# Attention scores of one unit split into products of 64 and of 16 contraction lanes

## The chip, the core and the metric

The kernel runs on one core of a Trainium2 chip. The metric is the device time of one execution in microseconds (us), the median of several runs. Five engines work beside each other, each with its own queue: TensorE (PE, matrix products; PEld is its weight load), VectorE (DVE), ScalarE (ACT), GpSimd (POOL) and SyncE (SP, which issues DMAs). Products land in PSUM, in banks of 512 float32 for each of the 128 partitions.

## What is computed

Routed attention, followed by a gated feed-forward layer. Queries, keys and values have 4 batches, 8 heads, 768 positions and 64 lanes. Each query and each key belongs to the nearest of 16 centroids of its head, and a query sees only keys of its own cluster:

```python
q_assign = np.argmax(np.einsum('bhsd,hcd->bhsc', q_n, c_n), axis=-1)
k_assign = np.argmax(np.einsum('bhsd,hcd->bhsc', k_n, c_n), axis=-1)
mask = q_assign[:, :, :, None] == k_assign[:, :, None, :]
scores = scale * np.matmul(q, k.transpose(0, 1, 3, 2))
scores = np.where(mask, scores, -1000000000.0)
scores = scores - np.max(scores, axis=-1, keepdims=True)
attn = np.exp(scores)
attn = attn / (np.sum(attn, axis=-1, keepdims=True) + 1e-09)
return np.matmul(attn, v).astype(np.float32)
```

The result, 3072 tokens of 512 lanes, is scaled by its root mean square and a weight, then goes through `silu(x @ w_gate) * (x @ w_val) @ w_out` with 1536 inner lanes.

## The kernel before

**The mask is inside the product.** A head's queries and keys are kept transposed as bf16, lanes on partitions, in the tiles `qext` and `kext`: 64 partitions (`D`) hold the lanes and the next 16 (`NC`) a one-hot vector of the cluster, so `KR = D + NC` = 80 partitions are contracted. The keys are divided by `ZS` = 2048 beforehand. So a query and a key of the same cluster get 1 added to their product, and the exponential, with scale `scale * ZS` and bias `off` = `-scale * ZS`, takes the 1 away where the clusters agree and leaves a very negative number where they don't.

**Units.** The work is cut into 8 units (`UNITS`, `NU` = 8), each one batch and one half of its queries: `UQ` = 384 query columns, all 8 heads, all 768 keys. `NU - 2` is number 6, the seventh.

**Scores.** `scores(u, h, i)` (L304) makes two of the six key blocks of 128 keys for one head; three calls make a head, 24 a unit. It takes a PSUM tile `s` of two banks (the pool `ps_s` has 2 such tiles), and for each bank issues one product with 128 keys as the stationary operand and 384 queries as the moving one (L314). One exponential on ScalarE (L318) then reads both banks and writes two blocks of `pT` in bf16.

**What follows.** `pv(u, h)` (L322) multiplies `pT` with the values and a column of ones (18 products of 65 columns, tile `acc`), and VectorE divides by the sum. The feed-forward of a unit runs one or two units later: `xtrans` (L371, tile `tx`), `gv` (L382, tiles `gate` and `val`, 4 products of 384 columns each), `out_mm` (L411, tile `o`, products of 512 columns).

**Order.** The order on each queue is written out by hand (`manual_schedule`). `attention` (L603) goes through the 24 score calls of a unit. After each call it puts what is due: the `pv` of the head before at a head's second call, squares for the norm in the last head, and pieces of a list `fill` in proportion to their estimated cost, so that TensorE has other products between two score calls. For the seventh unit the list holds the end of the feed-forward of unit 4, the output products of unit 4, and the first part of the feed-forward of unit 5; no group of heads is prepared any more. The first score call of each unit is followed by the second at once.

**Cluster products.** `cluster_products` (L235) multiplies queries or keys with the centroids in float32 for four heads; each product fills 32 of the array's columns and writes 32 partitions of the tile `sc` (L240). They occur up to the sixth unit.

**Names in the views.** `s` scores, `pT` exponentials, `acc` attention output, `gate`/`val`/`o` feed-forward, `tx` transposes of its input, `tq` transposes of queries and keys, `sc` cluster products.

Of the kernel before, what the change touches and what calls it, by code (L numbers as in the profile page):

```python
# [22 lines left out]
def kernel(  # L23
# [12 lines left out]
    nc = tc.nc  # L36
    B, H, S, D = q.shape
# [3 lines left out]
    P = 128  # L41
    ST = S // P
    HT = ST // 2
# [4 lines left out]
    NU = len(UNITS)  # L48
# [3 lines left out]
    KR = D + NC  # L52
# [55 lines left out]
    qext = [const.tile([P, HG, S], BF16, name=f"qext{i}") for i in range(4)]  # L108
    kext = [const.tile([P, HG, S], BF16, name=f"kext{i}") for i in range(4)]
# [38 lines left out]
    for i in range(P // 32):  # L148
        r = slice(32 * i, 32 * i + 32)
# [64 lines left out]
    def cols(of, g, e, a=0, b=UQ):  # L214

        return of.rearrange("p (x e) -> p x e", e=2)[:, a:b, e] if g < H // HG else of[:, e * UQ + a:e * UQ + b]
# [87 lines left out]
    def scores(u, h, i):  # L304
        b, col, nt = UNITS[u]
        g, hh, w = b * 2 + h // HG, h % HG, nt * P
        if i == 0:
            pT[u, h] = ptp.tile([P, ST, UQ], BF16, tag="pT", name="pT")
        n = ST // nt
        ps = ps_s.tile([P, 2, 512], F32, tag="s", name="s")  # L310
        flat = ps.rearrange("p a b -> p (a b)")
        for j in range(n):
            kc = n * i + j
            nc.tensor.matmul(ps[:, j, :w] if nt == HT else flat[:, j * w:(j + 1) * w],  # L314
                             lhsT=cols(kext[g % 4][:KR, hh], g, kc // HT, kc % HT * P, (kc % HT + 1) * P),
                             rhs=cols(qext[g % 4][:KR, hh], g, col // HT, 0, w), start=True, stop=True)
        of = ps[:, :, :w] if nt == HT else flat[:, :n * w].rearrange("p (c w) -> p c w", w=w)
        nc.scalar.activation(pT[u, h][:, n * i:n * i + n, :w], of, ACT.Exp, bias=off, scale=scale * ZS)  # L318
# [116 lines left out]
    def group_work(g):  # L435

        t, c = [], []
        for h in range(HG):
            n = g * HG + h
            t += [(0.3, lambda h=h: trans(g, h, 0)), (0.3, lambda h=h: trans(g, h, 1))]  # L440

            def others(n=n):
                vcast(n)
                load_qk(n + NQ)
                load_v(n + NV)

            def both(h=h, f=others):
                cast(nc.gpsimd, g, h, 0)
                f()
                cast(nc.vector, g, h, 1, (0,))  # L450
            if g == 2:
                c.append((0.0, others))
            else:
                c += [(0.0, both), (0.0, lambda h=h: cast(nc.vector, g, h, 1, (1,)))]
        a = []
        for m in range(2):
            a += [(0.0 if i else 0.7, f) for i, f in enumerate(cluster_steps(g, m))]
            if g <= 3:
                a.append((0.0, lambda m=m: place(nc.sync if g == 2 else nc.gpsimd, g, m)))
        if g > 3:  # L460
            a.append((0.0, lambda: [place(nc.gpsimd, g, m) for m in range(2)]))
        return t, c, a
# [17 lines left out]
    def ffn_work(u):  # L480
        n = UNITS[u][2] / HT
        w = [(0.18 * n, lambda c=c: xtrans(u, c)) for c in range(CC)]
        for f in range(FC):
            for val in (False, True):
                w.append((0.64 * n, lambda f=f, val=val: gv(u, f, val)))
        return w

    def out_work(u):
        return [(0.86, lambda t=t, p=p: out_mm(u, t, p)) for t in range(UNITS[u][2]) for p in range(3)]
# [113 lines left out]
    def attention(heads, fill, skip=0, hooks={}):  # L603
        gaps = [(u, h, i) for u, h in heads for i in range(UNITS[u][2])]
        total, done, n = sum(c for c, _ in fill), 0.0, 0
        for at, (u, h, i) in enumerate(gaps):
            scores(u, h, i)
            if i == min(1, UNITS[u][2] - 1):
                for p in due:
                    pv(*p)  # L610
                due[:] = [(u, h)]
            if h == H - 1:
                squares(u, i, False)
            if (u, h, i) in hooks:
                hooks[u, h, i]()
            while n < len(fill) and at >= skip and done <= total * (at + 1 - skip) / (len(gaps) - skip):
                done += fill[n][0]
                fill[n][1]()
                n += 1
        for _, f in fill[n:]:  # L620
            f()

    attention([(0, h) for h in range(H)], [], hooks={(0, *divmod(i, HT)): first.get(i, more) for i in range(H * HT)})
    for u in range(1, NU):
        ffn, o, g = ffn_work(u - 1), out_work(u - 2) if u > 1 else [], u + 2
        if u == 1:
            t, c, a = group_work(2)
            t3, c3, a3 = group_work(3)
            n = 4
# [61 lines left out]
```

## Time and profile before

| | |
|---|---|
| median of 3 runs | 354.11 us (354.07 to 354.23) |
| the profiled execution | 354.17 us |
| its span, first to last instruction | 352.4 us |
| mean granted TensorE clock | 0.995 |
| start of the first score of the seventh unit | 237.88 us |
| start of the first score of the eighth unit | 274.25 us |
| score products, all units | 384, of 80 lanes and 384 columns |
| exponentials | 192, 904 ns each |

A busy time counts an engine as busy from the start of an instruction to its end. Products on TensorE are pipelined, so one begins while the one before still drains: the duration of one (about 325 ns for 384 columns) is longer than the distance from one start to the next. A line of the groups gives the source line, engine and operation, written tile and read tiles, the shapes as partitions x elements with their type, how many there are, then their busy time, the mean duration of one in ns, and the idle time of the engine just before them with what ended it. A line of the timeline gives start, length from the first start to the last end, and then the same names.

### The profile page before, as it was taken

How to read it: one execution, taken by the hardware profiler on the slowest of the kernel's cores; microseconds unless marked ns; L12 is line 12 of the kernel's file. 1: busy time of each engine (PE TensorE's matmuls, PEld its weight loads, DVE VectorE, ACT ScalarE, POOL GpSimd, SP SyncE). 2: the span in 40 equal slices, each digit the busy share in tenths (PEclk: the TensorE clock that was granted, in tenths of full speed). 3: DMA queues.
4: the chain of work that ended last, by engine and by line, in shares of the span. 5: the costliest groups of instructions: out<-in, count | busy, mean ns of one | idle time of the engine just before them, and what ended most of it. 6: DMA issues, size and time to landing. Idle time of an engine off the chain costs nothing.

```text
span 352.4 us, 7991 instructions
## 1 busy us (share of the span) xinstructions
PE 340.9 (97%) x3028; PEld 210.2 (60%) x3045; DVE 223.1 (63%) x553; ACT 261.6 (74%) x459; POOL 110.2 (31%) x222
## 2 busy tenths in 40 slices
PE   8996999999999999999999999999999999999996
PEld 4544755664665656655576556756566656665653
DVE  4888678777457755686457863687456654666330
ACT  5995877986787777887688877978778887764421
POOL 4999168340542702444033711327000000000000
PEclk9998999999999999999999999999999999999999
DMA  7999959454253012610140011000010001001002
GB/s 270 368 206 171 274 141 250 139 172 146 74 175 95 24 59 86 192 34 16 60 123 2 17 38 60 2 2 23 32 61 0 2 33 60 2 1 62 30 2 89
DMA packets 27158, 31.62 MB, mean 90 GB/s; under 512 B 4464, under 2 KB 24176, under 8 KB 27120
## 3 DMA queue, kind: packets, MB, share of 16 engines
q1 hardware_dynamic: 18464, 25.02, 21.3%
q0 software_dynamic: 8368, 5.71, 9.9%
q8 instruction: 24, 0.39, 0.5%
q10 hardware_dynamic: 288, 0.39, 0.3%
q14 instruction: 14, 0.11, 0.1%
HBM read 28.35 MB, written 6.29 MB: 98 GB/s over the span
## 4 chain that ended last, share of the span: by engine, by line
PE 85%; DVE 7%; ACT 5%; issue 1%; POOL 0%; DVEq 0%; ACTq 0%; POOLq 0%
PE gate L390 17%; PE o L415 17%; PE val L390 16%; PE s L314 16%; PE acc L332 9%; PE tq L206 5%; PE sc L240 3%; ACT pT L318 3%; PE tx L377 1%; PE warm L117 1%; DVE kext L225 1%; ACT xn L357 1%; DVE qext L298 1%; DVE kext L298 1%; ACT th L398 1%
## 5 line engine op out<-in xcount | busy, mean ns | idle before, releaser
L318 ACT ACTIVATE pT<-s,off 128x768 bf16<-128x768 f32 x192 | 170.9, 904 | 38.0 <-PE s L314 36.8
L314 PE MATMUL s<-qext,kext 80*128 80x384 bf16 x384 | 95.1, 329 | 2.4 <-ACT pT L318 1.5
L399 DVE SCALAR_TENSOR_TENSOR th<-th,gate 128x384 f32<-128x384 f32 x84 | 46.4, 552 | 51.5 <-ACT th L398 51.4
L390 PE MATMUL gate<-xnT,wg 128*128 128x384 bf16 x384 | 78.3, 325 | 0.5 <-DVE gvT L403 0.4
L390 PE MATMUL val<-xnT,wv 128*128 128x384 bf16 x384 | 78.1, 326 | 0.0
L415 PE MATMUL o<-wo,gvT 128*128 128x512 bf16 x259 | 66.0, 379 | 0.9
L225 POOL CAST qext<-qkT 64x384 bf16<-64x384 f32 x64 | 34.1, 540 | 76.6 <-ACT qkT L212 37.3
L314 PEld LDWEIGHTS <-kext 80*128 80x128 bf16 x384 | 37.1, 99 | 33.4 <-issue 8.1
L398 ACT ACTIVATE th<-gate 128x384 f32<-128x384 f32 x84 | 41.1, 489 | 15.3 <-PE gate L390 14.9
L390 PEld LDWEIGHTS <-wv 128*128 128x128 bf16 x384 | 36.1, 97 | 25.1 <-issue 3.4
L390 PEld LDWEIGHTS <-wg 128*128 128x128 bf16 x384 | 35.9, 97 | 24.9 <-issue 3.4
L403 DVE SCALAR_TENSOR_TENSOR gvT<-th,val 128x384 bf16<-128x384 f32 x84 | 46.1, 549 | 7.2 <-PE val L390 2.6
L332 PEld LDWEIGHTS <-pT 128*128 128x128 bf16 x1152 | 43.9, 98 | 9.8 <-DVE x L339 1.1
L332 PE MATMUL acc<-vbf,pT 128*128 128x65 bf16 x1152 | 46.0, 194 | 0.7 <-DVE x L339 0.7
L415 PEld LDWEIGHTS <-gvT 128*128 128x128 bf16 x276 | 25.8, 97 | 25.1
L206 PE MATMUL tq<-ident_f,qk 128*128 128x128 f32 x192 | 31.4, 284 | 2.2 <-DVE qkT L210 2.1
L206 PEld LDWEIGHTS tq<-ident_f,qk 128*128 128x128 f32 x192 | 23.8, 145 | 8.8 <-DVE qkT L210 2.5
L212 ACT ACTIVATE qkT<-tq 128x384 f32<-128x384 f32 x56 | 26.1, 497 | 3.6 <-PE tq L206 3.0
L281 POOL DMA_DIRECT2D qext<-oh x40 | 19.1, 487 | 30.3 <-DVE oh L270 24.2
L378 DVE TENSOR_SCALAR xnT<-tx,gcol 128x384 bf16<-128x384 bf16 x32 | 11.9, 413 | 24.3 <-PE tx L377 24.3
L418 ACT COPY o_sb<-o 128x512 f32<-128x512 f32 x23 | 13.5, 585 | 17.4 <-PE o L415 17.4
L281 POOL DMA_DIRECT2D kext<-oh x40 | 19.1, 485 | 11.0 <-DVE oh L270 11.0
(74 smaller groups left out, 254.7 us busy)
## 6 DMA issues: line engine op xcount, KB each, us to landing
qk<-in_q_dram SPq DMA_DIRECT2D x32, 192.0 KB, 4.0
vs<-in_v_dram SPq DMA_DIRECT2D x32, 192.0 KB, 4.2
out_dram<-o_sb SPq DMA_DIRECT2D x23, 256.0 KB, 2.0
qk<-in_k_dram SPq DMA_DIRECT2D x30, 192.0 KB, 4.1
wg<-in_moe_w_gate_dram POOLq DMA_DIRECT2D x4, 384.0 KB, 7.0
wv<-in_moe_w_val_dram POOLq DMA_DIRECT2D x4, 384.0 KB, 8.7
wo<-in_moe_w_out_dram POOLq DMA_DIRECT2D x3, 512.0 KB, 5.6
qext<-oh POOLq DMA_DIRECT2D x40, 12.0 KB, 1.6
```

What stands on the lines that cost most here:

```text
L206: nc.tensor.transpose(ps[:, i * P:(i + 1) * P], qk[:, part, 2 * i:2 * i + 2].rearrange("p t d -> p (t d)"), ident_f)
L212: nc.scalar.activation(to, ps, ACT.Copy, scale=by)
L225: on.tensor_copy(to, of)
L281: on.dma_start(out=ext[D:D + NC, h, e * UQ:(e + 1) * UQ], in_=put[g, m][32 * h + e * NC:32 * h + (e + 1) * NC])
L314: nc.tensor.matmul(ps[:, j, :w] if nt == HT else flat[:, j * w:(j + 1) * w], lhsT=cols(kext[g % 4][:KR, hh], g, kc // HT, kc % HT * P, (kc ...
L318: nc.scalar.activation(pT[u, h][:, n * i:n * i + n, :w], of, ACT.Exp, bias=off, scale=scale * ZS)
L332: nc.tensor.matmul(acc[:, h % 2, t], lhsT=pT[u, h][:, kc, t * P:(t + 1) * P], rhs=vbf[g % 4][:, hh, kc % HT * 2 + kc // HT], start=kc == 0 ...
L390: nc.tensor.matmul(ps, lhsT=w[:, c, f * P:(f + 1) * P], rhs=xnT[u][:, c, :n], start=c == 0, stop=c == CC - 1)
L398: nc.scalar.activation(th, ps, ACT.Tanh, scale=0.5)
L399: nc.vector.scalar_tensor_tensor(th, th, 1.0, ps, op0=ALU.add, op1=ALU.mult)
L403: nc.vector.scalar_tensor_tensor(gvT[u][:, f, :n], gates[u], 0.5, ps, op0=ALU.mult, op1=ALU.mult)
L415: nc.tensor.matmul(outs[u], lhsT=gvT[u][:, f, t * P:(t + 1) * P], rhs=wo[:, f], start=f == 0, stop=f == FC - 1)
```

## The change

In `scores`, the seventh unit's products are taken apart along the contracted lanes. Where one product contracted all 80 partitions for a bank, there are now two that accumulate in it: one over partitions 0 to 63 (the lanes), one over 64 to 79 (the clusters). The order of the four products of a call alternates between the banks: lanes into bank 0, clusters into bank 1, then clusters into bank 0, lanes into bank 1. The first two clear their banks, the last two add. All other units keep the two products of 80 partitions. The operands, the PSUM tile and the exponential are the same.

```diff
         ps = ps_s.tile([P, 2, 512], F32, tag="s", name="s")
         flat = ps.rearrange("p a b -> p (a b)")
-        for j in range(n):
+        if u == NU - 2:
+            for a, b in ((0, D), (D, KR)), ((D, KR), (0, D)):
+                for j, r in enumerate((slice(*a), slice(*b))):
+                    kc = n * i + j
+                    nc.tensor.matmul(ps[:, j, :w], lhsT=cols(kext[g % 4][r, hh], g, kc // HT, kc % HT * P, (kc % HT + 1) * P),
+                                     rhs=cols(qext[g % 4][r, hh], g, col // HT, 0, w), start=a[0] == 0, stop=a[0] != 0)
+        for j in range(n if u != NU - 2 else 0):
             kc = n * i + j
```

## The prediction

> **What bounds the kernel now.** I read the page from the top, then only the stretch in which the seventh unit (u = 6, the number that `NU - 2` names) runs. First the busy shares and the slices:
>
> ```profile
> PE 340.9 (97%) x3028; PEld 210.2 (60%) x3045; DVE 223.1 (63%) x553; ACT 261.6 (74%) x459; POOL 110.2 (31%) x222
> PE   8996999999999999999999999999999999999996
> PE 85%; DVE 7%; ACT 5%; issue 1%; POOL 0%; DVEq 0%; ACTq 0%; POOLq 0%
> ```
>
> TensorE is full in nearly every slice and is 85% of the chain that ended last. A busy TensorE need not be at its peak, so I look at start times. The scores of the seventh unit start at 237.88 us and those of the eighth at 274.25 us. The table of windows for nearly this stretch, and the groups in it with shapes kept apart:
>
> ```profile
> 237.80:274.20 36.40, 36.24 (x335) 22.57 (x337) 21.94 (x55) 29.24 (x52) 6.85 (x15) 1.00 0.08 28
> L318 ACT ACTIVATE pT<-s,off 128x768 bf16<-128x768 f32 x25 | 22.3, 901 | 3.8 <-PE s L314 3.7
> L314 PE MATMUL s<-qext,kext 80*128 80x384 bf16 x48 | 11.7, 325 | 0.0
> L314 PEld LDWEIGHTS <-kext 80*128 80x128 bf16 x49 | 4.7, 98 | 3.7
> ```
>
> The columns of the first line are length, then busy time of PE, PEld, DVE, ACT and POOL, the granted clock, DMA share and GB/s. PE is busy 36.24 of 36.40 us at full clock; ACT has 7 us free and waits 3.7 us for the scores. So here an extra nanosecond on TensorE is an extra nanosecond of the span. The 325 ns of a score product is latency. What it costs is the distance to the next start, which the timeline shows:
>
> ```profile
> 240.45 0.49 PE L314 MATMUL s<-qext,kext 80*128 80x384 bf16 x2
> 240.78 0.81 PE L390 MATMUL gate<-xnT,wg 128*128 128x384 bf16 x4
> 241.43 0.81 PE L390 MATMUL val<-xnT,wv 128*128 128x384 bf16 x4
> ```
>
> Two scores take 0.33 us, four gates 0.65 us: 162 ns for each product of 384 columns, whether 80 or 128 lanes are filled. Neither the unit's 24 score calls nor what stands around them shows a gap worth naming, except two waits for ScalarE: 71 ns between the first two calls, and the larger one at the border to the eighth unit:
>
> ```profile
> 274.25 0.49 PE L314 MATMUL s<-qext,kext 80*128 80x384 bf16 x2
> 275.00 0.48 PE L314 MATMUL s<-qext,kext 80*128 80x384 bf16 x2 [0.26 <-ACT pT L318]
> ```
>
> Start to start it is 587 ns where 167 would do, so 420 ns are lost there. The chain runs over ACT from 270.70 to 274.96 us.
>
> The last view is the nearest thing to the change: the cluster products (L240), which use 32 of the array's columns at a time.
>
> ```profile
> 230.84 0.49 PE L314 MATMUL s<-qext,kext 80*128 80x384 bf16 x2
> 231.26 0.85 PE L240 MATMUL sc<-qkT,cblk 128*32 128x384 f32 x8
> 232.04 0.82 PE L390 MATMUL val<-xnT,wv 128*128 128x384 bf16 x4
> 232.70 0.49 PE L314 MATMUL s<-qext,kext 80*128 80x384 bf16 x2
> ```
>
> The single start times say more. Four of the eight start 6 to 7 ns apart and run together. From the last score to the first cluster product it is 253 ns instead of 162: 91 ns for going in. From the last cluster product it is 418 ns to the next gate or val product, where one such pass takes 326: 92 ns for coming out, and the product after that follows at 173 instead of 162, 11 ns more. The weight load of the first product on each side starts only 2 to 4 ns ahead of it; elsewhere it starts a whole product earlier. Float32 isn't the cause: from scores to the float32 transposes (L206) it is 161 ns, and from these to scores 109, their own pitch.
>
> **What the Trainium skill says.** "TensorEngine Tiling (Array Packing)", Tiling Modes, Key Properties: changing the tiling mode, not just the tile, drains TensorE. It lists tiles of 64 rows and of 32 rows as different modes, and 128 rows as a third. The trace agrees for columns (91 and 92 ns); for rows it shows nothing. "TensorE: Matmul & The Clock Gate", Part 3, says that products in different row groups run concurrently, starting about 4 ns apart; the trace shows this for column groups of one size (6 to 7 ns). The tiling page's Gotcha 1 (PSUM Pressure) says that different row tiles must not write one PSUM bank at the same time, which fits the alternation of banks in the change. The TensorE page, LDWEIGHTS: a load takes its time by columns, not by lanes. No form in the trace tests that; the 80-lane loads last 98 ns and the 128-lane ones 97.
>
> **The change part by part.** Before, a call issues two products of 80 lanes, one for each bank. Now it issues four: 64 lanes into bank 0, lanes 64 to 79 into bank 1, lanes 64 to 79 into bank 0, 64 lanes into bank 1. There are 24 calls: 8 heads of 3.
>
> - Passes. 48 products become 96, each still 384 columns wide. If they run one after another: 2 more of 162 ns = 324 ns a call.
> - Switches. 80 lanes fill more than 64 rows, so these scores run in the mode of the gate products (162 ns apart, no drain). 64 lanes ask for tiles of 64 rows, 16 lanes at 64 for tiles of 32. A call then goes 128, 64, 32, 32, 64, 128: four switches. None of this kind is in the trace. Bounds: 0 if rows need no drain, 103 if each costs what leaving the column mode costs with its slower second product. I take 91 for going in, 92 for each of the two inside, 103 for coming out: 378 ns a call.
> - Sum for a call: 702 ns; for 24 calls 16.85 us. The first two calls of the unit follow each other directly, in one mode, so one way out and in falls away: 194 ns. That leaves 16.66 us.
> - Weight loads: 48 more of about 98 ns. Behind a running product of 162 ns they cost nothing; at a switch the cover is gone, and the 91 to 103 ns measured there already contain it.
> - Waits. No wait is added in kind: the first product of a call waits for the exponential two calls before, as now. That exponential ended at least 594 ns ahead in all calls but the second. Everything later on TensorE's queue moves by the sum; ACT's exponential starts later with it and has slack. A slower call removes the 71 ns. In the last head, two calls after 270.70 us each give ACT 0.7 us more to catch up, so the 420 ns at the border vanish too. Together 0.49 us comes back; next late would again be the stream on TensorE.
> - No DMA, VectorE or GpSimd instruction changes; SP's and POOL's queues are not touched.
>
> 16.66 - 0.49 = 16.2 us. The profiled execution took 354.17 us (span 352.4, with 1.8 around it), which gives 370.4. The median of the runs is 354.11, so 370.3 us.
>
> **Rivals.**
> 1. Both row sizes count as one tiled mode and run together. Each pair then takes one pass plus about 7 ns, and only the ways in and out cost: 14 + 194 = 208 ns a call, 4.99 us in all, less 0.19 for the adjacent calls and 0.45 of waits: 4.35 us, 358.5 us. For it: concurrency in the cluster products, and the TensorE page's row groups. Against it: the sizes differ, and those products are of one size.
> 2. One mode, but no overlap: 324 + 194 = 518 ns a call, 12.43 - 0.19 - 0.49 = 11.75 us, 365.9 us. For it: score products of both sizes still stream from one queue in order. Against it: the column groups of the cluster products do overlap, and the TensorE page says the same of row groups.
> 3. No overlap, no drain for rows: 324 ns a call, 7.78 - 0.49 = 7.3 us, 361.4 us. For it: 80 lanes next to 128 cost nothing. Against it: both are 128-row work.
> 4. Not slower: the two row groups run together, and no drain is paid for row tiles. The place is the score call, and the price is about 14 ns a call: 0.34 us less some 0.1 of waits, 354.3 us, no change. It decides as long as the switches of a call stay under about 22 ns together: 24 x (14 + 22) = 0.86 us, less 0.02 for the adjacent calls and 0.14 of waits, is the 0.7 us that can be told from no change. A clear gain has little to come from: even perfect pairs leave two passes a call, as before, and the two waits hold 0.49 us in all. Against it: the 91 and 92 ns at the column mode.
>
> **How the numbers follow.** The forecast, serial with four switches, gets 0.50. Its own range is 367 (60 ns inside a call and at its ends instead of 92: 24 x 4 x 32 ns = 3 us less) to 371.5. Rival 1 gets 0.20, rival 2 0.10, rival 3 0.07, rival 4 0.08; 0.05 is left for switches dearer than any here. The range from 358.0 to 371.8 holds the forecast and rivals 1 to 3 and leaves out 0.13 or so. Differences under 0.2% (0.7 us) can't be told from none. Rival 4 is the only source of same or faster: 0.06 same, 0.02 faster, and 0.92 slower.
>
> **What would show it.** In the profile after, the score line should have 96 products in two forms, 64 and 16 lanes, in the seventh unit. Serial with switches: starts about 254 ns apart inside a call except the middle pair at 162, and a weight load only a few nanoseconds ahead of its product. Rival 1: starts in pairs a few nanoseconds apart, then a pass. Rival 2: all at 162 inside the call, with 91 and 92 ns at its ends. Rival 3: 162 everywhere. The seventh unit should last 36.4 + 16 us, the eighth begin without its wait, and the other units stay as they are. The prediction is wrong if two row groups start together, or if changing from 64 to 32 rows costs nothing.

## The result, and the profile after

The changed kernel takes 371.09 us (370.86 to 372.12, 4 runs) against 354.10 us for the kernel before: a ratio of 1.0485 (of the means of the runs), with a 95% interval from 1.0465 to 1.0504. The profiled execution took 371.13 us with a span of 369.3 us at a mean clock of 0.995, so the two profiles differ by 16.9 us.

The lines of the page that answer to those shown of before:

```profile
PE 358.1 (97%) x3076; PEld 211.1 (57%) x3093; DVE 223.2 (60%) x553; ACT 262.8 (71%) x459; POOL 110.0 (30%) x222
PE   8996999999999999999999999999999999999996
PE 87%; DVE 7%; ACT 4%; issue 1%; POOL 0%; DVEq 0%; ACTq 0%; POOLq 0%
```

The time went to TensorE alone: 17.2 us more busy time, about what the span grew by, against 1.2 us at ScalarE and 0.2 us or less at VectorE and GpSimd. A page like this can't say whether TensorE streams or drains, since both count as busy. The seventh unit, with shapes kept apart, says more (first its window, columns as before; then its groups):

```profile
237.89:291.53 53.64, 53.48 (x382) 23.30 (x385) 22.48 (x55) 30.65 (x52) 6.67 (x15) 1.00 0.06 19
L324 ACT ACTIVATE pT<-s,off 128x768 bf16<-128x768 f32 x25 | 22.4, 900 | 17.7 <-PE s L316 17.7
L316 PE MATMUL s<-qext,kext 64*128 64x384 bf16 x48 | 15.8, 333 | 0.0
L316 PE MATMUL s<-qext,kext 16*128 16x384 bf16 x48 | 11.9, 326 | 0.0
```

53.64 us where it was 36.37, so 17.27 us more. The exponentials are the same (900 ns each), but ScalarE now waits 17.7 us for the scores instead of 3.7. One call in the timeline of TensorE, and below it the weight loads of the same stretch:

```profile
240.91 0.81 PE L396 MATMUL val<-xnT,wv 128*128 128x384 bf16 x4
241.66 1.02 PE L316 MATMUL s<-qext,kext 64*128 64x384 bf16 x4
242.61 0.66 PE L396 MATMUL gate<-xnT,wg 128*128 128x384 bf16 x3
```

```profile
241.65 0.09 PEld L316 LDWEIGHTS <-kext 64*128 64x128 bf16 x1 [0.32 <-issue]
241.92 0.11 PEld L316 LDWEIGHTS <-kext 16*128 16x128 bf16 x2 [0.17 <-issue]
242.34 0.09 PEld L316 LDWEIGHTS <-kext 64*128 64x128 bf16 x1 [0.32 <-issue]
242.61 0.44 PEld L396 LDWEIGHTS <-wg 128*128 128x128 bf16 x4 [0.17 <-issue]
```

From the first score to the first gate product it is 0.95 us, where a call took 0.33. The loads come in four groups with idle time before each: at each change of row size the load waits, and only within a size (the two of 16 lanes, or the gates) does the next one go ahead. Start to start in this call, in ns, from the last val product on: 259 to 64 lanes, 265 to 16, 173 to 16, 253 to 64, 265 to the gate product, 173 to the next. All 162 would be a stream without drains. The same row of numbers stands in all calls, within 2 ns, except where products of another width (512, 128 or 65 columns) come before or after, and in the first two calls, which follow each other directly.

At the border to the eighth unit the wait for ScalarE has nearly gone, as the second call follows without a bracket:

```profile
291.54 0.88 PE L320 MATMUL s<-qext,kext 80*128 80x384 bf16 x4
```

Its two calls are 230 ns apart instead of 587: 0.36 us came back. 17.27 - 0.36 is the 16.9 us of the span.

### The profile page after: what moved, and what is told of

The parts are those of the page before. It is cut to its first block, busy times and chain, and to the rows that moved or that the text cites. A ratio compares the mean times of both kernels' runs of the same rounds, so it can differ in the third digit from the quotient of the medians.

```text
span 369.3 us, 8079 instructions
## 1 busy us (share of the span) xinstructions
PE 358.1 (97%) x3076; PEld 211.1 (57%) x3093; DVE 223.2 (60%) x553; ACT 262.8 (71%) x459; POOL 110.0 (30%) x222
## 4 chain that ended last, share of the span: by engine, by line
PE 87%; DVE 7%; ACT 4%; issue 1%; POOL 0%; DVEq 0%; ACTq 0%; POOLq 0%
PE gate L396 16%; PE val L396 16%; PE o L421 16%; PE s L320 13%; PE acc L338 9%; PE s L316 6%; PE tq L206 5%; PE sc L240 3%; ACT pT L324 2%; PE tx L383 2%; PE warm L117 1%; DVE kext L225 1%; DVE qext L298 1%; DVE kext L298 1%; PE o L432 1%
## 5 line engine op out<-in xcount | busy, mean ns | idle before, releaser
L320 PE MATMUL s<-qext,kext 80*128 80x384 bf16 x336 | 83.3, 330 | 2.1 <-ACT pT L324 1.3
L320 PEld LDWEIGHTS <-kext 80*128 80x128 bf16 x336 | 32.5, 99 | 29.4 <-issue 7.6
L424 ACT COPY o_sb<-o 128x512 f32<-128x512 f32 x23 | 13.5, 585 | 17.7 <-PE o L421 17.7
L316 PE MATMUL s<-qext,kext 64*128 64x384 bf16 (+1 forms) x96 | 24.4, 329 | 0.0
```

Source lines behind the costliest of these rows:

```text
L316: nc.tensor.matmul(ps[:, j, :w], lhsT=cols(kext[g % 4][r, hh], g, kc // HT, kc % HT * P, (kc % HT + 1) * P), rhs=cols(qext[g % 4][r, hh], ...
```

## The experiments

Nine kernels were run. All but the last differ from the changed kernel in the products of a seventh-unit call, four of them also in zeros written ahead. A whole time also carries what varies elsewhere in the kernel (the kernel before had medians from 354.10 to 354.46 us in these comparisons, and single runs up to 355.99). Part of that lies in the first unit: it takes 29.0 to 29.1 us at a mean granted clock of 0.88 in the profiles of the reordered pieces, of the cluster products together and of the second run of two of 64, and 27.9 to 28.1 us at 0.94 in all others. So I judge most of them by the seventh unit's length in the profile, from its first score to the eighth unit's first; it is 36.37 us before and 53.65 in the changed kernel.

**The pieces in another order.** Three changes of size a call instead of four. (In these diffs `a` and `b` bound the partitions, `j` is the bank, `first` clears it.)

```diff
-for a, b in ((0, D), (D, KR)), ((D, KR), (0, D)):
+for a, b, j, first, last in ((0, D, 0, True, False), (0, D, 1, True, False), (D, KR, 1, False, True), (D, KR, 0, False, True)):
```

> The four products of a seventh-unit call in the order 64 lanes bank 0, 64 lanes bank 1, 16 lanes bank 1, 16 lanes bank 0: the same four products, one change of row size fewer in a call (128-64-32-128). Theory (a change of row size drains TensorE, about 102 ns each with the slower product after it): 2 extra passes 324 ns + 3 x 102 = 630 ns a call, 15.1 us, less 0.1 for the adjacent first calls and 0.4 of waits that go: 368.7 us. Rival (the cost sits with each partial product, whose weight load is not covered): as the changed kernel, 371.1 us.

Measured: 369.35 us, ratio 1.0419 (1.0393 to 1.0445), which is 14.8 us on 354.1; the seventh unit lasts 51.27 us, 2.4 us less than in the changed kernel. Between the two products of one size it is 173 ns; at each change, next to products of 384 columns, 253 to 259:

```profile
243.31 0.92 PE L315 MATMUL s<-qext,kext 64*128 64x384 bf16 x4
244.16 0.82 PE L395 MATMUL gate<-xnT,wg 128*128 128x384 bf16 x4
```

0.85 us from first score to gate, against 0.95 with the same four products. The cost goes with the number of changes, not with the number of pieces.

**The banks one after the other.**

```diff
-for a, b in ((0, D), (D, KR)), ((D, KR), (0, D)):
+for a, b, j, first, last in ((0, D, 0, True, False), (D, KR, 0, False, True), (D, KR, 1, True, False), (0, D, 1, False, True)):
```

> The four products in the order 64 lanes bank 0, 16 lanes bank 0, 16 lanes bank 1, 64 lanes bank 1: the sizes follow each other as in the changed kernel, the banks no longer alternate. Theory (row size alone): no difference, 371.1 us within 0.5. Rival (the alternation of banks, or adding in a bank right after another product, makes the gaps): the two inner gaps of 92 ns move or go, 2 x 24 x 0.1 = 4.8 us, so 366 us or 376 us.

Measured: 371.23 us, ratio 1.0475 (1.0451 to 1.0499); the seventh unit lasts 53.65 us, and its starts are those of the changed kernel within 2 ns (259, 266, 173, 253, 266, 173). The alternation of the banks does nothing here, neither good nor bad.

**The cluster lanes alone.** Two changes of size and no further pass.

```diff
-for a, b in ((0, D), (D, KR)), ((D, KR), (0, D)):
+for a, b, j, first, last in ((D, KR, 0, True, True), (D, KR, 1, True, True)):
```

> Two products of 16 lanes a call in the seventh unit, one for each bank; the 64 lanes of queries and keys are left out there, so all keys of a cluster weigh the same in that unit. No extra pass, two changes of row size a call. Theory: 2 x 102 x 24 = 4.9 us, less 0.2 for the adjacent first calls and 0.4 of waits: 358.4 us. Rival (the cost needs two partial products added in one bank): no change, 354.1 us.

Measured: 358.83 us, ratio 1.0122 (1.0102 to 1.0141), 4.3 us on 354.1; the seventh unit lasts 40.90 us.

```profile
240.65 0.49 PE L315 MATMUL s<-qext,kext 16*128 16x384 bf16 x2
241.08 0.82 PE L395 MATMUL gate<-xnT,wg 128*128 128x384 bf16 x4
```

Two products of 16 lanes take 0.43 us to the gate product, where two of 80 lanes take 0.33. Starts: 258, 173, 253, 173. So a way in and a way out cost 96 + 11 and 91 + 11 = 209 ns over the pitch of 162, with nothing accumulated and no piece added. A 16-lane pass streams no faster than an 80-lane one: where the first two calls follow each other, 16-lane products start 162 ns apart.

**Twice the products, all of 80 lanes.** Two further passes and weight loads a call, no change of size; the second pair repeats the first.

```diff
-for a, b in ((0, D), (D, KR)), ((D, KR), (0, D)):
+for a, b, j, first, last in ((0, KR, 0, True, True), (0, KR, 1, True, True), (0, KR, 0, True, True), (0, KR, 1, True, True)):
```

> Four products of 80 lanes a call in the seventh unit, bank 0, bank 1, bank 0, bank 1, each of the second pair overwriting the first with the same values: two extra passes and two extra weight loads a call, no change of row size. Theory: 324 ns a call, 7.8 us less 0.5 of waits: 361.4 us, all starts 162 to 167 ns apart. Rival (any extra product with its weight load costs what the partial ones cost): as the changed kernel, 371.1 us.

Measured: 361.78 us, ratio 1.0210 (1.0188 to 1.0231), 7.4 us on 354.1; the seventh unit lasts 44.10 us, 7.73 more than before.

```profile
241.12 0.81 PE L315 MATMUL s<-qext,kext 80*128 80x384 bf16 x4
241.78 0.81 PE L395 MATMUL gate<-xnT,wg 128*128 128x384 bf16 x4
```

Four products take 0.66 us to the gate product, 162 to 167 ns each. The two further weight loads of a call cost nothing visible. The passes are 7.7 of the changed kernel's 17.3 us in this unit; the other 9.5 come with the changes of size.

**Two row groups of one size, and of two sizes.** The changed kernel can't tell whether its two row groups failed to overlap because they never do or because their sizes differ. The Trainium skill ("TensorEngine Tiling (Array Packing)", Gotcha 1) has it that different row tiles must not write one bank at the same time; no run here tries that. So these runs leave the accumulation out: one product of 64 lanes into bank 0, one over partitions from 64 on into bank 1, so that each bank lacks what the other has. In one kernel the second has 16 rows, in the other 64, of which 48 are zeros, so both compute the same.

```diff
-for a, b in ((0, D), (D, KR)), ((D, KR), (0, D)):
+for a, b, j, first, last in ((0, D, 0, True, True), (D, P, 1, True, True)):
+        for t in (kext[2], qext[2], kext[3], qext[3]):
+            nc.gpsimd.memset(t[D:], 0.0)
```

In the run with 16 rows `KR` stands in place of `P`.

> Two products a call in the seventh unit: lanes 0 to 63 into bank 0, and partitions 64 to 127 (16 cluster partitions and 48 of zeros, cleared earlier by GpSimd) into bank 1; the clusters of even key blocks and the lanes of odd ones are left out. Both have 64 rows, so one row size with two row groups. Theory (products of one row size but different row groups run together; only a change of size drains): starts a few ns apart, one pass a call fewer, two changes of size: -162 + 7 + 204 = 49 ns a call, 1.2 us less 0.2 and up to 0.2 of waits: about 355 us. Rival (row groups never overlap): 204 ns a call, 358.4 us.

> As the run of two products of 64 rows, but the second has the 16 cluster partitions alone, without the zeros: the same row groups' start, bank and values, a smaller row size. Theory: three changes of size and no overlap: 3 x 102 = 306 ns a call, 7.3 us less 0.1 for the adjacent first calls and 0.4 of waits: 360.9 us. Rival (different row groups overlap whatever their sizes, and something else made the gaps in the changed kernel): as the run of two products of 64 rows, 355 to 358 us.

Measured: 359.37 us (ratio 1.0141, 1.0126 to 1.0155) and 364.16 us (1.0274, 1.0259 to 1.0288), 4.4 and 3.3 us over what was expected. The extra time doesn't lie in the seventh unit, which lasts 37.26 and 43.48 us as the theory had it (36.37 + 0.9, + 7.1). It lies in the second: 36.0 us in the run of two of 64 instead of 32.16 (the third is unchanged). Four memsets of zeros, 2.65 us each, follow one another on GpSimd, and one VectorE instruction of the norm lasts until the last of them ends. In the run of two of 64, and last in the kernel before:

```profile
42.63 2.65 POOL L596 MEMSET qext<- 64x3072 bf16 x1
43.14 2.16 DVE L125 TENSOR_SCALAR half<-ms 128x3 int32<-128x3 int32 x1
```

```profile
43.34 0.17 DVE L125 TENSOR_SCALAR half<-ms 128x3 int32<-128x3 int32 x1
```

TensorE waits 3.1 us for that norm, against 0.3 before. The clock granted in the unit is 0.95 instead of 1.00, and TensorE's busy time there rises from 31.22 to 32.46 us, which makes up the rest. So I ran both again with the zeros elsewhere: one tile at the start, three where GpSimd waits for that norm.

```diff
+    nc.gpsimd.memset(kext[2][D:], 0.0)
+                for t in (qext[2], kext[3], qext[3]):
+                    nc.gpsimd.memset(t[D:], 0.0)
                 nc.gpsimd.tensor_copy(idle, xn[0][:, HT - 1, DM - 1:])
```

> The two products of 64 rows a call in the seventh unit again (clusters of even key blocks and lanes of odd ones left out), with the zeros written while GpSimd waits for other engines, since in the earlier run they held up its casts and a stretch of the second and third units. Theory (products of one row size overlap, a change of size drains): the seventh unit lasts 37.3 us as in that run, all others as in the kernel before; 0.9 us more, less about 0.2 of the wait at the border to the eighth unit: 354.8 us. Rival (part of what was lost there belongs to the split): 356 us or more again.

> The same zeros at the same places, but the second product has the 16 cluster partitions alone. Theory (64 and 16 are different row sizes, each change drains): the seventh unit lasts 43.5 us, 7.1 us more than before, less 0.4 of waits: 360.8 us, 6 us above the run of two products of 64 rows. Rival (overlap whatever the sizes): no more than 1 us between the two.

Measured: 358.47 us (ratio 1.0112, 1.0074 to 1.0151) and 364.05 us (1.0294, 1.0246 to 1.0342). The whole times missed again, by 3 to 4 us: in the run of two of 64 the first score of the whole kernel starts at 13.68 us instead of 11.48, and the first unit is 1 us longer. The late start goes back to the zeros, as a VectorE cast that takes 0.23 us before is held until the memset at the start ends at 4.70 us:

```profile
2.04 2.66 POOL L290 MEMSET kext<- 64x3072 bf16 x1
2.40 2.38 DVE L152 CAST ident<-ident_f 128x128 bf16<-128x128 f32 x1
```

The centroids come later, and TensorE waits 1.2 us for them; what makes the rest of the 2.2 us was not taken apart. The longer first unit can't be put down to the zeros: at the same clock of 0.88 it is as long in two runs that write none. The norm's instruction is held again, for 0.61 us in the run of two of 64 and 1.71 us in that of 64 and 16, and the second unit is 0.45 and 1.55 us longer, about what the instruction lost (0.44 and 1.54). The seventh unit again lasts 37.26 and 43.48 us. Timeline of the run of two of 64, then of 64 and 16:

```profile
244.12 0.34 PE L316 MATMUL s<-qext,kext 64*128 64x384 bf16 x2
244.39 0.82 PE L396 MATMUL gate<-xnT,wg 128*128 128x384 bf16 x4
```

```profile
243.63 0.60 PE L316 MATMUL s<-qext,kext 64*128 64x384 bf16 x2
244.16 0.82 PE L396 MATMUL gate<-xnT,wg 128*128 128x384 bf16 x4
```

Two products last 0.34 us from the first start to the last end when both have 64 rows; one alone lasts 0.33. They start 3 ns apart, and the gate follows 0.27 us after: one pass and one drain. With 64 and 16 rows, the second starts 265 ns after the first, and the gate 0.53 us after the first: two passes, two drains. The weight loads of the two of 64 rows (first run) start together as well:

```profile
244.15 0.10 PEld L315 LDWEIGHTS <-kext 64*128 64x128 bf16 x2 [0.32 <-issue]
244.41 0.44 PEld L395 LDWEIGHTS <-wg 128*128 128x128 bf16 x4 [0.17 <-issue]
```

These two kernels differ in the rows of the second product alone. So the row groups at partitions 0 and 64 do overlap when both have 64 rows, each with its own bank; with 16 rows next to 64 they don't, and zeros that make them 64 bring the overlap.

**A use of it: fewer changes of mode in the kernel before.** The kernel before changes mode around its cluster products. In this run those of a group's queries and keys stand next to each other for groups 4 to 7.

```diff
+            a = [(1.4, lambda x=a[0][1], y=a[4][1]: (x(), y()))] + a[1:4] + a[5:]
             a.append((0.0, lambda: [place(nc.gpsimd, g, m) for m in range(2)]))
```

> The kernel before, with the cluster products of the queries and those of the keys of a group put next to each other for groups 4 to 7 instead of apart. Each group then goes into the 32-column mode and out of it once instead of twice. Theory: 91 + 92 + 11 = 194 ns less on TensorE for each of 4 groups, 0.78 us: 353.3 us. Rival (VectorE or a buffer of the shared PSUM pool, which two cluster products now hold at once, is late): no change or up to 1 us slower, 354.1 to 355 us.

Measured: 354.82 us, ratio 1.0008 (0.9997 to 1.0018): no gain. Half of the changes did go: sixteen cluster products stand in one block, 1.43 us to the next score where two blocks took 0.785 each to the product after them.

```profile
150.84 1.50 PE L240 MATMUL sc<-qkT,cblk 128*32 128x384 f32 x16
152.27 0.50 PE L314 MATMUL s<-qext,kext 80*128 80x384 bf16 x2
```

But the unit around it lasts 41.02 us instead of 41.04. At its end, in this run and then in the kernel before:

```profile
156.41 0.49 PE L314 MATMUL s<-qext,kext 80*128 80x384 bf16 x2
157.17 0.48 PE L314 MATMUL s<-qext,kext 80*128 80x384 bf16 x2 [0.26 <-ACT pT L318]
```

```profile
155.80 0.88 PE L314 MATMUL s<-qext,kext 80*128 80x384 bf16 x4
```

The two calls at the border are 586 ns apart, where the kernel before has 231. TensorE arrives earlier and waits for ScalarE's exponential. So it is at each border from the fourth unit to the seventh (584 to 587 ns against 230 to 235). The third unit, whose border had 588 ns already, is 0.37 us shorter, and the seventh, which has no cluster products, is 0.35 us longer: what a unit saves is waited away at the next border. The rival had named VectorE or the buffers; the late one is ScalarE. At these borders TensorE and ScalarE are close to even, so a saving would have to be made on both, which was not tried.

## Why the prediction was right

**Row size is a tiling mode, and a change drains.** The forecast took this from the Trainium skill ("TensorEngine Tiling (Array Packing)", Tiling Modes) and its price from the cluster products. That a change between row sizes costs what the column mode costs was taken on trust, as nothing in the trace before showed one. It holds. With four products a call the seventh unit lasts 53.65 us at four changes, 51.27 at three and 44.10 at none; with two products it lasts 40.90 at two changes and 36.37 at none. What fills the 91 to 96 ns of a change isn't shown: "drains" is the page's word, and the trace shows that the next weight load starts only after them. A rival is the uncovered weight load itself, which is about as long. Against it, the two lengths don't go together: into the column mode the load takes 106 ns and the change 91, into 64 rows it is 92 and 96. No run here varies the load alone.

**The passes.** 324 ns a call were taken; the run with doubled 80-lane products gives 7.73 us for the unit, and 24 x 324 ns less the 71 ns wait is 7.71. Weight loads, which the forecast took to go by columns and not by lanes, last 90 to 94 ns with 16 lanes in the changed kernel, and nearly all of those with 128 lanes 95 to 99.

**The switches.** This is the one term that was small. 378 ns a call were taken: 91, 92, 92, and 103 for the last, the 11 ns of a slower second product counted once. In the trace a call has 96, 103, 11, 91, 104 and 11 ns over the pitch of 162: the 11 ns come after each change, and the way in from 128 rows is 96 instead of 91. That is 416, and 8 ns of it a call had before (its second product followed at 167, the next but one at 165): 408 net. 24 x 30 ns are the missing 0.7 us. It is a small miss of size; the four switches themselves are all there.

**The waits.** 0.49 us was to come back. The 71 ns between the first two calls went; of the 420 ns at the border 357 went, and 63 stayed. The forecast let the whole wait vanish because the last two calls give ScalarE 1.4 us more; they do, but the eighth unit's calls are 230 ns apart rather than 167, as those of the sixth unit were before. What holds these last 63 ns was not tried.

**Overlap across sizes,** which the first rival needed, didn't occur: the reason given against it, that the sizes differ, is now measured on both sides (3 ns apart at 64 and 64, 265 at 64 and 16). The second and third rivals put no cost on a change inside a call. They fall with the start times of the changed kernel and again with the reordered run, where one change fewer takes away about 100 ns a call. The fourth falls with the cluster lanes alone, where the drains stand by themselves.

So 16.2 us were forecast and 16.9 measured between the profiles; the rest of the difference to 371.09 is the spread of the runs.

## What to carry to other kernels

On a full TensorE, splitting a contraction by lanes costs whole passes, as a pass of 384 columns took 162 ns here with 16, 80 or 128 lanes alike. Before products of 64 or fewer rows are put among products of 128, count the changes of row size: each was worth about 100 ns here, more than half a pass of 384 columns. If row groups are to overlap, give them one size, if need be with zero rows, and a bank each, as in the runs that overlapped. Overlap alone needn't pay: with two products of 64 rows a call saved 159 ns and paid about 200 for its two changes, and the seventh unit lasted 37.26 us instead of 36.37. And look at the other engines' lateness before a saving on TensorE is counted.

## What was not expected

- After a change of mode the second product of 384 columns starts 173 ns after the first instead of 162 (265 instead of 254 where it is a change itself), in every run with such a change unless the two overlap, for row modes as for the 32-column one. The weight load of the first starts only 2 to 5 ns ahead of it, and that of the second about 15 ns after the first load.
- Zeros cost more than the drain they were to show. A GpSimd memset of 64 partitions x 3072 bf16 lasts 2.65 us, and in each of the four runs one to three VectorE instructions that overlap a memset last until it ends (2.16 instead of 0.17 us, 2.38 instead of 0.23), while the other 17 to 20 that start during the memsets keep their length within 0.05 us. What tells them apart was not tried. TensorE then waits for VectorE, and the whole time grows by 3 to 4 us in either placing, of which 1 us in the second run of two of 64 is the longer first unit that runs without zeros have too.
